# One product of weights with float32 operands, and float64 weights converted by a scale

## The chip, the cores and the metric

The kernel runs on one core of a Trainium2 chip. The metric is the device time of one execution in microseconds (us). It was executed three times for its time, and once more under the hardware profiler.

## What is computed

Causal attention with a bias from a running sum (4 batches, 8 heads, 576 positions, head dimension 64), then a gated layer, then a layer whose second half is normalised and mixed over positions:

```python
x = softmax(scale * q @ k.T + bias) @ v          # 32 heads, gathered to (4, 576, 512)
gate = sigmoid(conv over 5 positions of x)       # conv_w
x = (gate * (x @ w_val)) @ w_out                 # both 512 x 512
h = relu(x @ w_in)                               # w_in is 512 x 1024
u, v = h[..., :512], h[..., 512:]
out = (u * (w_spatial @ normalise(v) + b)) @ w_out2
```

Nothing stands between `w_out` and `w_in`, so the kernel computes the 512 x 1024 product w_out @ w_in once, on the chip, and uses it in place of the two. This product is called the fold here. The weight matrices w_val, conv_w, w_out, w_in and w_out2 arrive as float64 and are converted to float32 on the chip; q, k, v and the rest are float32.

## The kernel before, in words

**Order of the work.** The main loop (in the part of the code that is printed below only where it touches the change) goes over the 32 heads. For each head `scores` makes q.k in float32 (heads 0 to 7) or from split operands (heads 8 to 31), VectorE (DVE, L253) adds the mask and finds the row minimum, ScalarE (ACT, L258) takes the exponential, TensorE (PE) transposes the result (`transposes`), and `pv` multiplies by v for two heads at a time. Between these pieces the loop calls `more`, which takes the next steps from a queue: conversion of weights, the fold, and the two mixing layers of a batch, `mixing_a` and `mixing_b`. Within one engine instructions run in a fixed order. A scheduler that runs when the program is built sets this order; it is not written out by hand.

**Split operands.** A float32 matrix is split in a high part in a shorter format (`hi_of`, L93, mostly on ACT) and the rest (`lo_of`, L100, on DVE or POOL). A product then takes three matmuls per block of 128 rows, high by high, low by high and high by low (`three`, L440).

**Conversion of a float64 piece** (`from_f64`, L388). A piece is 128 x 512 numbers of 64 bits, 512 KB. A transfer issued on the SP queue brings it as pairs of 32-bit words. ACT (L404) takes the absolute value of the upper word, read as float32, times 65536. DVE clamps it (L405), masks the sign out of the upper word (L406), and shifts and joins (L407). GpSimd (POOL) scales the lower word (L410) and adds (L411). There are 20 such pieces, four each of w_out, of the two halves of w_in, of w_val and of w_out2, and one small one of conv_w.

**The fold.** `fold_prep` (L415) converts a piece of w_out (j is None) or of half j of w_in and splits it: `wo_h`, `wo_l`, `wih`, `wil`, one ACT instruction and one DVE instruction each. The two halves of w_in share one buffer for each part. `fold(ec, j)` (L452) makes a 128 x 512 block of the product by `three`, 12 matmuls, and splits it into `wch` and `wcl`. There are eight such blocks. Half 1 is prepared in heads 2 to 6 and multiplied in heads 7 to 9, half 0 is multiplied in heads 13 and 14.

**What sets the pace around the change.** `first_steps` (L653) puts the steps in order: conv_w, w_out, half 1 of w_in, w_val, then the four folds of half 1; `second_steps` prepares half 0 next to `mixing_b(0)`; `third_steps` prepares w_out2 and w_spatial. Loads of later heads, of weights and of weight blocks written back to memory all go through the SP queue in order.

Of the kernel before, what the change touches and what calls it, by code (L numbers as in the profile page):

```python
# [7 lines left out]
F32 = mybir.dt.float32  # L8
F32R = mybir.dt.float32r
I32 = mybir.dt.int32  # L10
U32 = mybir.dt.uint32
AF = mybir.ActivationFunctionType
ALU = mybir.AluOpType
# [3 lines left out]
NATIVE = 8  # L17


F64_LOW = 2.0 ** (896 // 8 - 127 + 16)  # L20
F64_HIGH = 2.0 ** (1150 // 8 - 127 + 16) * (1.0 + 6.0 / 8 + (1.0 - 2.0 ** -20) / 8)


@with_exitstack
def tile_stickbreak_attention_moe(
# [22 lines left out]
    NP = H // 2  # L48
# [16 lines left out]
    V, G, A, SY = nc.vector, nc.gpsimd, nc.scalar, nc.sync  # L65
# [21 lines left out]
    def f(ap):  # L87
        return ap.bitcast(F32)

    def hi_of(eng, out_, in_):  # L90

        if eng is A:
            A.activation(out_, in_, AF.Copy)  # L93
        elif eng is G:
            G.tensor_scalar(out=out_, in0=in_, scalar1=1.0, scalar2=1.0, op0=ALU.mult, op1=ALU.mult)
        else:
            V.tensor_copy(out_, in_)

    def lo_of(eng, out_, in_, hi):
        eng.tensor_tensor(out=out_, in0=in_, in1=f(hi), op=ALU.subtract)  # L100
# [21 lines left out]
    for c in (0, 128):  # L122
        n = 128 if c == 0 else 64
# [30 lines left out]
    def tmp(name, dt=F32):  # L154
        return mid.tile([128, S], dt, tag="tmp", name=name, bufs=2)
# [129 lines left out]
    def evac_split(dst_hi, dst_lo, src):  # L285
        A.activation(dst_hi, src, AF.Copy)
        lo_of(V, dst_lo, src, dst_hi)
# [45 lines left out]
    def conv(b, p):  # L333
# [5 lines left out]
        for k in range(3, -1, -1):  # L339
# [7 lines left out]
    wtmp = wtmp_cm.__enter__()  # L347
# [7 lines left out]
                         op1=ALU.max)  # L355
# [11 lines left out]
    SY.dma_start(cum_d[:, 0, :], f(ch))  # L367
    SY.dma_start(cum_d[:, 1, :], f(cl))

    wo_h = wtmp.tile([128, NP, 512], F32R, name="wo_h")  # L370
    wo_l = wtmp.tile([128, NP, 512], F32R, name="wo_l")
    wi = {}


# [10 lines left out]
                return fn(*a)  # L385
        return g

    def from_f64(src, n):  # L388

        k = count[0] % 5  # L390
        count[0] += 1
        if count[0] <= 13 and k < 3:
            if k == 0 and "g" not in W:
                W["g"] = mid.tile([128, NP * (2 * S + 64)], I32, tag="g", name="wg")
            r = W["g"][:, k * 1536:k * 1536 + 1024]
            a = f(W["g"][:, k * 1536 + 1024:k * 1536 + 1536])
        else:
            r = mid.tile([128, 1024], I32, tag="wr", name="wr", bufs=2)
            a = tmp("wa")
        W["r"] = r  # L400
        r, a = r.rearrange("p (c t) -> p c t", t=2)[:, 0:n, :], a[:, 0:n]
        SY.dma_start(r, src.rearrange("p (c t) -> p c t", t=2))
        up, low = r[:, :, 1], r[:, :, 0]
        A.activation(a, f(up), AF.Abs, scale=65536.0)  # L404
        V.tensor_scalar(out=a, in0=a, scalar1=F64_HIGH, scalar2=F64_LOW, op0=ALU.min, op1=ALU.max)  # L405
        V.tensor_scalar(out=up, in0=up, scalar1=-2 ** 31, scalar2=None, op0=ALU.bitwise_and)  # L406
        V.scalar_tensor_tensor(out=up, in0=a.bitcast(I32), scalar=3, in1=up, op0=ALU.logical_shift_left,  # L407
                               op1=ALU.bitwise_or)

        G.tensor_scalar(out=low, in0=low.bitcast(U32), scalar1=2.0 ** -29, scalar2=None, op0=ALU.mult)  # L410
        G.tensor_tensor(out=a.bitcast(I32), in0=low, in1=up, op=ALU.add)  # L411
        return a

    @paced
    def fold_prep(kc, j):  # L415

        if j is None:
            wh, wl, src = wo_h, wo_l, woT[:, kc * 1024:(kc + 1) * 1024]
        else:
            if j not in wi:  # L420
                wi[j] = [wtmp.tile([128, NP, 512], F32R, tag=f"wi{x}", name=f"wi{x}") for x in "hl"]
            wh, wl = wi[j]
            src = w_in[:, kc, j * 1024:(j + 1) * 1024]
        t = from_f64(src, 512)
        hi_of(A, wh[:, kc, :], t)
        lo_of(V, wl[:, kc, :], t, wh[:, kc, :])

    @paced
    def weight_prep(src, dst, mc):
        t = from_f64(src[mc], 512)  # L430
        w = W["r"].rearrange("p (t c) -> p t c", t=2).bitcast(F32R)
        if dst is wv_d and mc < 2:
            w = mid.tile([128, 2, 4, 128], F32R, tag="wv", name="wv", bufs=2)
            AHEAD[False, 0, mc] = w[:, 0], w[:, 1]
            w = w.rearrange("p t k m -> p t (k m)")
        hi_of(A, w[:, 0, :], t)
        lo_of(V, w[:, 1, :], t, w[:, 0, :])
        SY.dma_start(dst[mc], f(w))

    def three(pt, kcs, hl_a, hl_b):  # L440

        n = len(kcs)
        for j, kc in enumerate(kcs):
            ah, al = hl_a(kc)
            bh, bl = hl_b(kc)
            T.matmul(pt, ah, bh, start=j == 0, stop=False)
            T.matmul(pt, al, bh, start=False, stop=False)
            T.matmul(pt, ah, bl, start=False, stop=j == n - 1)

    KC = list(range(NP))  # L450

    def fold(ec, j):  # L452
        pt = ps.tile([128, 512], F32, tag="m", name="psm", bufs=2)
        es = slice(ec * 128, (ec + 1) * 128)
        cs = slice(j * 512, (j + 1) * 512)
        three(pt, KC, lambda kc: (wo_h[:, kc, es], wo_l[:, kc, es]), lambda kc: (wi[j][0][:, kc, :], wi[j][1][:, kc, :]))
        evac_split(wch[:, ec, cs], wcl[:, ec, cs], pt)


# [193 lines left out]
    def first_steps():  # L653
        nonlocal cw
        cw = early.tile([128, NP, 5], F32, name="cw")
        V.tensor_copy(cw, from_f64(conv_w, 20).rearrange("p (c k) -> p c k", k=5))
        order = [(lambda mc=mc: weight_prep(w_val, wv_d, mc)) for mc in KC]
        order += [(lambda mc=mc: fold_prep(mc, None)) for mc in KC]
        order = order[4:] + [(lambda kc=kc: fold_prep(kc, 1)) for kc in KC] + order[:4]
        for o in order:  # L660
            o()
            yield
        for ec in range(4):
            fold(ec, 1)
            yield 2.56

    def second_steps():
        for kc in KC:
            fold_prep(kc, 0)
            yield  # L670
# [11 lines left out]
    def start():  # L682

        m = mixing_a(0)
        yield from both(m, first, 2)
        m = mixing_b(0)
        yield from both((next(m) for _ in range(5)), second_steps())
        for ec in range(4):
            fold(ec, 0)
            yield 2.56  # L690
        open_late()
        yield from both((next(m) for _ in range(8)), third_steps())
        yield from m
# [117 lines left out]
```

## Time and profile before

| | before |
|---|---|
| median of three executions | 500.99 us (500.11 to 503.02) |
| profiled execution, its own time | 502.31 us |
| its span in the trace | 500.5 us |
| PE busy | 474.9 us, 95% |
| DVE busy | 320.2 us, 64% |
| ACT busy | 315.4 us, 63% |
| POOL busy | 165.8 us, 33% |
| granted TensorE clock, mean | 0.993 of full speed |

The span is the profiled execution from its first to its last instruction; the profiled execution's own time is 1.81 us more than its span, and 1.32 us more than the median. Busy time of PE includes the time that a matmul takes to run through the array, so that its 95% is not 95% of what it could do. The trace is read here in stages that are cut where the scores of a head begin on PE: head 2 at 21.38 us, head 8 at 79.59, head 15 at 167.22, head 22 at 271.76 and head 31 at 379.71 us. In these stages the engines stand against each other in different ways, which the shares over the whole span do not show. PEclk is the granted clock, where 1.00 is TensorE's higher level, 2.4 GHz, and its lower level is 1.2 GHz.

### The profile page before, as it was taken

To read this page: it belongs to the slowest core of one execution; us is meant where nothing else is said; L and a number is where in the kernel's file an instruction comes from. 1 tells how busy PE (TensorE), PEld (TensorE's weight loads), DVE (VectorE), ACT (ScalarE), POOL (GpSimd) and SP (SyncE) were. 2 spreads that over 40 slices of the span, in tenths; PEclk is the share of its full clock that TensorE was granted. 3 is DMA by queue.
4 is the path that set the end of the run, shared out by engine and by line. 5 is a ranking of instruction groups with operands and counts; after the bars stand their busy time and mean duration, and the time that the engine had idled before them with its cause. 6 is when DMAs were issued, how large, how long until landed. Compare 5 with 4: busy or idle time off the path is not lost.

```text
span 500.5 us, 9139 instructions
## 1 busy us (share of the span) xinstructions
PE 474.9 (95%) x3138; PEld 400.7 (80%) x3138; DVE 320.2 (64%) x835; ACT 315.4 (63%) x796; POOL 165.8 (33%) x183
## 2 busy tenths in 40 slices
PE   8697789979999999999999999999999999999997
PEld 5453457768777898998879999888778989988997
DVE  5599999698989885655578476555794453124120
ACT  2787968786776876675577758674876624234322
POOL 5587452045583103103243023012342022136130
PEclk9898999999999999999999999999999999999999
DMA  3876477558383644287531412784510072600002
GB/s 93 223 250 209 108 256 252 158 158 236 118 265 113 182 128 123 76 252 231 145 88 43 130 47 80 230 249 129 168 42 28 0 279 54 211 1 2 0 13 84
DMA packets 51567, 68.23 MB, mean 136 GB/s; under 512 B 23936, under 2 KB 39456, under 8 KB 51520
## 3 DMA queue, kind: packets, MB, share of 16 engines
q1 hardware_dynamic: 46592, 62.84, 42.3%
q10 hardware_dynamic: 4928, 4.80, 2.9%
q8 instruction: 25, 0.41, 0.4%
q14 instruction: 22, 0.18, 0.1%
HBM read 54.91 MB, written 9.16 MB: 128 GB/s over the span
## 4 chain that ended last, share of the span: by engine, by line
PE 63%; DVE 20%; DMA 7%; ACT 3%; issue 3%; POOL 2%; SPq 1%; DVEq 0%; ACTq 0%; POOLq 0%
PE psm L75 45%; PE pso L75 5%; PE pst L75 5%; DVE p L253 4%; DVE z L341 3%; DMA wv<-wv_d 2%; PE pss L244 2%; DMA raw<-in_qk 2%; PE pss L245 2%; DVE v L583 2%; PE psw L75 1%; DVE qk L100 1%; DVE wg L407 1%; ACT p L258 1%; PE pss L242 1%
## 5 line engine op out<-in xcount | busy, mean ns | idle before, releaser
L258 ACT ACTIVATE p<-p,nm 64x64 f32<-64x64 f32 (+4 forms) x160 | 88.5, 554 | 22.6 <-DVE nm L253 22.2
L253 DVE CUSTOM_DVE_ANT_0 p<-pss,mask 64x64 f32<-64x64 f32 (+4 forms) x160 | 62.7, 412 | 25.1 <-PE pss L245 17.7
L301 ACT ACTIVATE pt<-pst 128x512 f32<-128x512 f32 (+2 forms) x128 | 59.0, 495 | 28.3 <-PE pst L75 28.1
L341 DVE SCALAR_TENSOR_TENSOR z<-x,cw,z 128x575 f32<-128x575 f32 (+1 forms) x64 | 57.3, 896 | 7.4 <-ACT z L338 7.1
L75 PE MATMUL pst<-ident,p 128*128 128x128 f32 x416 | 60.1, 276 | 2.0 <-ACT p L258 1.8
L100 POOL TENSOR_TENSOR y<-gt,y 128x288 fp32r<-128x288 f32 x32 | 27.1, 847 | 102.8 <-ACT y L93 102.8
L100 POOL TENSOR_TENSOR g<-gt,g 128x288 fp32r<-128x288 f32 x32 | 28.8, 903 | 95.0 <-ACT g L93 94.7
L75 PEld LDWEIGHTS pst<-ident,p 128*128 128x128 f32 x416 | 48.4, 141 | 11.2 <-ACT p L258 4.3
L75 PE MATMUL psm<-g,wch 128*128 128x288 f32 x256 | 55.1, 299 | 1.2 <-DVE wcl L100 0.9
L75 PE MATMUL pso<-pt,vraw 128*64 128x512 f32 (+4 forms) x320 | 52.1, 448 | 0.0
L75 PE MATMUL psm<-wch,g 128*128 128x512 f32 x144 | 47.7, 400 | 0.0
L244 PE MATMUL pss<-qk 128*64 128x64 f32 (+1 forms) x144 | 43.6, 320 | 2.7 <-DVE nm L253 2.3
L75 PEld LDWEIGHTS psm<-g,wch 128*128 128x128 f32 x256 | 42.4, 189 | 2.0 <-DVE wcl L100 1.2
L75 PE MATMUL psm<-y,wv 128*128 128x288 f32 x288 | 42.0, 297 | 0.5 <-ACT ot L629 0.5
L75 PE MATMUL psm<-xvh,wv 128*128 128x288 f32 x192 | 40.2, 300 | 1.7 <-DMA wv<-wv_d 1.3
L245 PE MATMUL pss<-kd,cn 66*64 66x64 f32 (+1 forms) x144 | 41.1, 294 | 0.0
L242 PE MATMUL pss<-raw 128*128 128x320 f32 (+4 forms) x96 | 31.5, 432 | 9.6 <-DVE nm L253 6.0
L75 PEld LDWEIGHTS psm<-y,wv 128*128 128x128 f32 x288 | 39.6, 188 | 0.9 <-ACT ot L629 0.7
L524 DVE TENSOR_TENSOR gt<-psm,u 128x288 f32<-128x288 f32 x32 | 14.5, 456 | 39.3 <-PE psm L75 31.2
L75 PEld LDWEIGHTS pso<-pt,vraw 128*64 128x64 f32 (+1 forms) x320 | 19.3, 138 | 23.4 <-issue 16.7
L75 PE MATMUL psm<-wsh,vh 128*128 128x288 f32 x128 | 38.0, 299 | 0.0
L75 PE MATMUL psm<-g,wcl 128*128 128x288 f32 x128 | 38.0, 297 | 0.0
(142 smaller groups left out, 1118.9 us busy)
## 6 DMA issues: line engine op xcount, KB each, us to landing
raw<-in_qk SPq DMA_DIRECT2D x24, 448.0 KB
wv<-wo_d SPq DMA_DIRECT2D x12, 512.0 KB
R<-r_d SPq DMA_DIRECT2D x32, 160.0 KB
wv<-wv_d SPq DMA_DIRECT2D x10, 512.0 KB
out<-ot ACTq DMA_DIRECT2D x32, 144.0 KB
vraw<-in_vp SPq DMA_DIRECT2D x32, 128.0 KB
cn<-qk SPq DMA_DIRECT2D x24, 144.0 KB
raw<-in_qk SPq DMA_DIRECT2D x48, 64.0 KB
```

The lines of the kernel that those rows point to most:

```text
L75: m = op(*a, **k)
L100: eng.tensor_tensor(out=out_, in0=in_, in1=f(hi), op=ALU.subtract)
L242: nc.tensor.matmul(pst[0:m, o:o + b - a], r[:, 1, q0:q0 + m], r[:, 0, k0 + a:k0 + b], start=True, stop=True)
L244: nc.tensor.matmul(pst[0:m, o:o + b - a], qa[:, q0:q0 + m], kb[:, k0 + a:k0 + b], start=True, stop=False)
L245: nc.tensor.matmul(pst[0:m, o:o + b - a], qc[0:KD, q0:q0 + m], kd[0:KD, k0 + a:k0 + b], start=False, stop=True)
L253: LAST["V"] = V.tensor_tensor_reduce(out=row[:, a:b], in0=src, in1=mask[0:m, o:o + b - a], scale=-0.125, scalar=3.0e38 if a == 0 else nm[0 ...
L258: A.activation(row, row, AF.Exp, bias=nm[0:m, i:i + 1], scale=-1.0, accum_out=sm[h // 2 % 2][0:m, h % 2, i:i + 1])
L301: A.activation(PT[h][:, to:to + n], pt[:, o:o + n], AF.Copy)
L341: V.scalar_tensor_tensor(out=z[:, d:], in0=x[:, :S - d], scalar=cw[:, p, k:k + 1], in1=z[:, d:], op0=ALU.mult, op1=ALU.add)
L407: V.scalar_tensor_tensor(out=up, in0=a.bitcast(I32), scalar=3, in1=up, op0=ALU.logical_shift_left, op1=ALU.bitwise_or)
L524: V.tensor_tensor(out=t, in0=psrc, in1=other, op=ALU.mult)
L583: V.tensor_scalar(out=v[0:m], in0=v[0:m], scalar1=mv[0:m, 0:1], scalar2=rs[0:m], op0=ALU.subtract, op1=ALU.mult)
```

## The change

The fold's operands stay float32, `wo_f` and `wi[j]`, with no split: each block of the product is made by 4 float32 matmuls in place of 12 on split operands. The two halves of w_in have a buffer each. A converted piece of these matrices is built directly in its place (`home`). In `from_f64`, for all 20 pieces, ACT multiplies the upper word by 2**-112 with its sign kept, and the clamp on DVE is gone: one DVE instruction masks and shifts, a second one joins the sign. POOL's two instructions and the transfers stay as they were.

```diff
-F64_LOW = 2.0 ** (896 // 8 - 127 + 16)
-F64_HIGH = 2.0 ** (1150 // 8 - 127 + 16) * (1.0 + 6.0 / 8 + (1.0 - 2.0 ** -20) / 8)
+F64_SCALE = 2.0 ** -(896 // 8)
...
-    wo_h = wtmp.tile([128, NP, 512], F32R, name="wo_h")
-    wo_l = wtmp.tile([128, NP, 512], F32R, name="wo_l")
+    wo_f = wtmp.tile([128, NP, 512], F32, name="wo_f")
...
-    def from_f64(src, n):
+    def from_f64(src, n, home=None):
...
-            a = tmp("wa")
+            a = tmp("wa") if home is None else None
+        if home is not None:
+            a = home
...
-        A.activation(a, f(up), AF.Abs, scale=65536.0)
-        V.tensor_scalar(out=a, in0=a, scalar1=F64_HIGH, scalar2=F64_LOW, op0=ALU.min, op1=ALU.max)
-        V.tensor_scalar(out=up, in0=up, scalar1=-2 ** 31, scalar2=None, op0=ALU.bitwise_and)
-        V.scalar_tensor_tensor(out=up, in0=a.bitcast(I32), scalar=3, in1=up, op0=ALU.logical_shift_left,
-                               op1=ALU.bitwise_or)
+        A.activation(a, f(up), AF.Copy, scale=F64_SCALE)
+        ai = a.bitcast(I32)
+        V.tensor_scalar(out=up, in0=ai, scalar1=0x0FFFFFFF, scalar2=3, op0=ALU.bitwise_and, op1=ALU.logical_shift_left)
+        V.scalar_tensor_tensor(out=up, in0=ai, scalar=-2 ** 31, in1=up, op0=ALU.bitwise_and, op1=ALU.bitwise_or)
...
     def fold_prep(kc, j):
...
-            wh, wl, src = wo_h, wo_l, woT[:, kc * 1024:(kc + 1) * 1024]
+            home, src = wo_f, woT[:, kc * 1024:(kc + 1) * 1024]
...
-                wi[j] = [wtmp.tile([128, NP, 512], F32R, tag=f"wi{x}", name=f"wi{x}") for x in "hl"]
-            wh, wl = wi[j]
-            src = w_in[:, kc, j * 1024:(j + 1) * 1024]
-        t = from_f64(src, 512)
-        hi_of(A, wh[:, kc, :], t)
-        lo_of(V, wl[:, kc, :], t, wh[:, kc, :])
+                wi[j] = wtmp.tile([128, NP, 512], F32, name=f"wi{j}")
+            home, src = wi[j], w_in[:, kc, j * 1024:(j + 1) * 1024]
+        from_f64(src, 512, home[:, kc, :])
...
-        three(pt, KC, lambda kc: (wo_h[:, kc, es], wo_l[:, kc, es]), lambda kc: (wi[j][0][:, kc, :], wi[j][1][:, kc, :]))
+        for kc in KC:
+            T.matmul(pt, wo_f[:, kc, es], wi[j][:, kc, :], start=kc == 0, stop=kc == NP - 1)
```

The scheduler sets a new order on every engine. Two places matter below. The rows give line, operation, result<-operands and shape, in the order of one engine; the line of a statement is up to four lower in the changed code (L253 is L252, L438 is L434).

**DVE at the end of head 2** (`p`, `nm` and `pss` belong to the scores; `wg`, `wr` and `wa` to a piece that is being converted; `wo_` to w_out). Before:

```order
L266 TENSOR_SCALAR den<-sm_121 128x10
L253 ISA p_125,nm<-pss,mask 128x256
L253 ISA nm 128x1
L268 RECIPROCAL rin<-den 128x10
L405 TENSOR_SCALAR wa<-wa 128x512
L406 TENSOR_SCALAR wr<-wr 128x512
L100 TENSOR_TENSOR wo_l<-wg,wo_h 128x512
L253 ISA p_125,nm<-pss,mask,nm 128x320
```

The same place with the change:

```order
L265 TENSOR_SCALAR den<-sm_121 128x10
L252 ISA p_125,nm<-pss,mask 128x256
L252 ISA nm 128x1
L267 RECIPROCAL rin<-den 128x10
L406 TENSOR_SCALAR wr<-wo_f 128x512
L407 SCALAR_TENSOR_TENSOR wr<-wo_f,wr 128x512
L252 ISA p_125,nm<-pss,mask,nm 128x320
```

Ahead of the last reduction of the head the clamp (L405) and the low part (L100) are gone, and the joining instruction (L407), which came behind that reduction before, has moved up.

**The SP queue around the second load of head 11** (`raw_67`). Before:

```order
L438 DMA wv_d<-wg 128x1024
L202 DMA cn_116<-qk 64x576
L175 DMA raw_67<-in_qk 128x2x448
L177 DMA raw_67<-in_qk 128x2x64
L178 DMA raw_67<-in_qk 128x2x64
```

With the change:

```order
L434 DMA wv_d<-wg 128x1024
L201 DMA cn_116<-qk 64x576
L402 DMA wr<-in_w_in 128x1024
L174 DMA raw_67<-in_qk 128x2x448
L176 DMA raw_67<-in_qk 128x2x64
```

The fourth and last load of half 0 of w_in now stands directly ahead of the load of this head; before, it came 15 entries later.

## Rows read from the trace of the kernel before

**Rows 1.** the page's head, busy us and slices of 12.5 us in tenths
```profile
PE 474.9 (95%) x3138; PEld 400.7 (80%) x3138; DVE 320.2 (64%) x835; ACT 315.4 (63%) x796; POOL 165.8 (33%) x183
...
PE   8697789979999999999999999999999999999997
...
DVE  5599999698989885655578476555794453124120
```

**Rows 2.** windows, all engines: stretch, length, busy (instructions), then clock, DMA share, GB/s
```profile
21.38:79.59 58.21, 49.92 (x249) 29.41 (x250) 55.54 (x145) 46.59 (x122) 38.06 (x27) 0.94 0.65 202
79.59:167.22 87.63, 81.94 (x500) 65.54 (x499) 77.92 (x196) 67.66 (x168) 36.70 (x33) 1.00 0.60 182
167.22:271.76 104.54, 103.33 (x739) 91.36 (x738) 68.14 (x177) 69.80 (x178) 25.23 (x30) 1.00 0.50 145
271.76:379.71 107.95, 106.94 (x766) 94.25 (x765) 70.35 (x200) 77.11 (x205) 25.15 (x30) 1.00 0.44 129
379.71:500.50 120.79, 117.17 (x837) 109.75 (x834) 35.88 (x79) 44.48 (x101) 30.01 (x40) 1.00 0.21 68
```

**Rows 3.** waits of PE, 21.38 to 79.59: us in total, times, longest
```profile
PE pss L242 <- DVE nm L253: 5.8, 8, 1.3
PE pss L242 <- DMA raw<-in_qk: 3.4, 1, 3.4
PE psq L75 <- ACT rt L275: 1.4, 1, 1.4
PE psr L75 <- DVE rin L268: 0.7, 1, 0.7
```

**Rows 4.** chain of waits, 0 to 160 us: start, us, what
```profile
27.02 0.73 DVE wa L405
...
28.10 0.60 DVE wo_l L100
28.70 0.46 DVE p L253
```

**Rows 5.** groups of DVE instructions, 21.38 to 79.59 us
```profile
L405 DVE TENSOR_SCALAR wg<-wg 128x512 f32<-128x512 f32 x7 | 4.3, 612 | 0.0
...
L405 DVE TENSOR_SCALAR wa<-wa 128x512 f32<-128x512 f32 x5 | 3.4, 672 | 0.2 <-ACT wa L404 0.2
...
L100 DVE TENSOR_TENSOR wil<-wg,wih 128x512 fp32r<-128x512 f32 x3 | 2.0, 680 | 0.0
...
L100 DVE TENSOR_TENSOR wo_l<-wg,wo_h 128x512 fp32r<-128x512 f32 x2 | 1.7, 844 | 0.0
...
L100 DVE TENSOR_TENSOR wo_l<-wa,wo_h 128x512 fp32r<-128x512 f32 x2 | 1.4, 679 | 0.0
...
L100 DVE TENSOR_TENSOR wil<-wa,wih 128x512 fp32r<-128x512 f32 x1 | 0.7, 672 | 0.0
```

**Rows 6.** timeline of PE in head 7: start, us, line, operation, tiles, count
```profile
71.39 1.09 PE L75 MATMUL pst<-ident,p 128*128 128x128 f32 x8
72.32 0.92 PE L242 MATMUL pss<-raw 128*128 128x448 f32 x2
72.72 0.75 PE L75 MATMUL psm<-wih,wo_h 128*128 128x512 f32 x1
...
75.61 0.40 PE L75 MATMUL psm<-wil,wo_h 128*128 128x512 f32 x1
```

**Rows 7.** windows, columns as in Rows 2
```profile
40.00:50.00 10.00, 7.83 (x34) 3.45 (x32) 10.00 (x27) 7.82 (x21) 7.56 (x6) 0.83 0.64 218
```

**Rows 8.** groups of DVE instructions, 79.59 to 271.76 us
```profile
L100 DVE TENSOR_TENSOR wil<-wa,wih 128x512 fp32r<-128x512 f32 x4 | 3.0, 745 | 1.8 <-PE pst L75 1.8
...
L405 DVE TENSOR_SCALAR wa<-wa 128x512 f32<-128x512 f32 x7 | 2.9, 419 | 1.0 <-ACT wa L404 1.0
```

**Rows 9.** tile wr: minimum/median/maximum ns of each group
```profile
L406 DVE TENSOR_SCALAR wr<-wr x10: 387/427/1265, 27.7 to 137.2; 128x512 int32<-128x512 int32 x10
```

**Rows 10.** groups of ACT instructions, 21.38 to 79.59 us
```profile
L93 ACT ACTIVATE wih<-wg 128x512 fp32r<-128x512 f32 x3 | 1.9, 617 | 0.0
```

## Prediction

> **What bounds the kernel now.** I read the page's busy shares first and then its slices. PE is busy 95% of the span, so PE looks like the bound everywhere; but in the slices PE is below 9 tenths in most of the first ten, and there DVE stands at 9 [rows 1]. The next view is the table of stages, cut at the heads. From head 2 to head 8 (58.21 us) PE is busy 49.92 us and idle 8.29, while DVE is busy 55.54. From head 8 to head 15 (87.63 us) PE is idle 5.69 and DVE busy 77.92. From head 15 to head 22 PE is idle 1.21 of 104.54 us, and from there to head 31 1.01 of 107.95 [rows 2]. So there are two regimes: until head 8 DVE sets the pace, from head 15 on PE does, and between them both nearly do. The waits of PE in the first stage say the same: 5.8 us on the row minimum that DVE makes, in 8 waits, 1.4 and 0.7 us on ACT and DVE steps of the sums; the 3.4 us on a load end where the stage begins and are none of its time [rows 3]. The chain of waits runs there from one DVE instruction to the next, and among them are the ones that this change removes: a clamp (L405) and a low part (L100) right ahead of a score's reduction (L253) [rows 4]. Since PE is the bound later, a microsecond that heads 2 to 15 arrive earlier is a microsecond off the end, and so is one that PE gets in addition.
>
> **What the change removes from DVE.** In the stage from head 2 to head 8 there are 12 clamps, 4.3 + 3.4 = 7.7 us, and eight low parts, 2.0 + 1.7 + 1.4 + 0.7 = 5.8 us [rows 5]: 13.5 of 55.54 us. From head 8 on there are seven clamps, 2.9 us, and four low parts, 3.0 us [rows 8]: 5.9 of 77.92 us. (One more clamp of full size lies ahead of head 2, and that of conv_w is 20 numbers wide; both count for nothing.) The two DVE instructions that stay are of the kinds that were there. The one that now masks and shifts took between 387 and 1265 ns, with 427 in the middle, in its old form [rows 9]; the new form has two operations and other operands, and the trace does not show it. I take the same price; if each of 20 ran at the upper end, that would be 20 x 0.84 = 17 us of DVE, nearly all that was saved, and if each ran at the lower end, 1 us less. The middle is nearest, for it is the same kind of instruction, one input and no second tensor.
>
> **What it removes from ACT and POOL.** ACT loses twelve high parts of 0.617 us [rows 10], 7.4 us in all; two thirds lie in the first stage, where ACT is busy 46.59 of 58.21 us [rows 2]. It is not the longest there, so I count nothing for this by itself: the cover is DVE and PE, and if both got shorter than ACT, ACT's 42 us would still not be the longest. POOL's work is the same. Its last add now ends a piece, while before an ACT and a DVE instruction followed; no one waits for the pieces in the first stage, so this is counted at nothing too.
>
> **What it adds on PE.** Twelve split matmuls of 512 columns become four float32 ones. Of the split ones, the first ends at 72.72 + 0.75 = 73.47 us and the twelfth at 75.61 + 0.40 = 76.01; between them are 11 steps, so one is 0.231 us and a block 2.77 [rows 6]. A float32 matmul shows as two records. The one of 448 columns just ahead ends at 72.32 + 0.92 = 73.24, and the transposes before it at 71.39 + 1.09 = 72.48: 0.76 us, for 512 columns 0.87, for a block of four 3.47 [rows 6]. So a block costs 0.70 us more, eight of them 5.6. If a float32 matmul took four steps of 0.231, it would be 0.92, a block 3.70 and eight blocks 7.4 us more. A gain is excluded, as 3.47 is the lowest that the float32 rows give. I take 5.6, from the row of the same type of operand. Two blocks (1.4 us) come ahead of head 8, as before, and six (4.2 us) in the next stage. There the extra evacuation is none: ACT and DVE split a block into wch and wcl as before.
>
> **What is moved.** The last load of half 0 of w_in now stands on SP directly ahead of a load of head 11, behind which further loads queue. It waits for POOL to free a buffer. POOL was busy 36.70 of 87.63 us in that stage [rows 2] and takes that piece a head earlier than before, so I count nothing; without that cover a late load costs PE what the one of head 2 did, 3.4 us [rows 3]. The halves of w_in no longer share a buffer, so the second half's pieces need not wait for the folds of the first. That can only spread work.
>
> **The sum.** In the first stage PE can get back 8.29 us of idle time, and some time of its clock: between 40 and 50 us the granted clock is 0.83, a loss of 1.7 us [rows 7], after PE had waited again and again. That is 10.0 us. DVE's relief of 13.5 us is more than this, but PE also waits on round trips, from score to reduction and back, that a free DVE shortens and does not remove. I take 60%, 6.0 us, less 1.4 for two blocks: -4.6. In the second stage 5.69 us of idle time stand against 5.9 us of relief on DVE; I take half, 2.8, less 4.2 for six blocks: +1.4. After that PE has no idle time worth counting and the work is the same: 0. Together -3.2 us. The profiled execution took 502.31 us, 1.32 above the median, so it would take 499.1, and the median would be 500.99 - 3.2 = **497.8 us**.
>
> **A rule that speaks against it.** By the span's row PE is the busiest engine, at 95% against 64% of DVE [rows 1]. The Trainium skill, Perfetto Trace Analysis, section Identifying the Most-Contended Engine, says to improve the engine with the highest occupancy first; a change that loads that engine to relieve a lesser one goes against this. By that rule none of the idle time comes back, and the time would be 500.99 + 5.6 = 506.6 us; by the stages it is 497.8. The trace bears the rule out from head 15 on, and not before head 8. The same page's section Optimization Strategy grants that the most-contended engine can change over time.
>
> **The rivals.**
> - *PE pays and gets little back* (slower). PE's waits on the row minimum are round trips between engines and not a backlog of DVE, and the freed time goes idle on DVE. For it: DVE waited only little for anything, yet in the second stage PE is busy 81.94 of 87.63 us with 4.2 us added. Against it: DVE's 55.54 of 58.21 us [rows 2]. It decides if less than 3.1 of the 15.7 us (10.0 + 5.7) come back; with none, 506.6, with 2 us, 504.6.
> - *The gain and the price cancel* (within 0.5%). Between 3.1 and 8.1 us come back, as when loads on SP and ACT's 42 us take the place of DVE after the first few microseconds. With half of the first stage's idle time without its clock, 4.1, and a third of the second's, 1.9: 500.99 + 5.6 - 6.0 = 500.6.
> - *DVE was the whole bound* (faster). All of 10.0 us come back in the first stage and 4 in the second: 500.99 + 5.6 - 14.0 = 492.6. For it: the chain through DVE alone [rows 4].
> - That the change does not do what it says is excluded by the order of DVE: clamps and low parts are gone from it.
>
> **How the numbers follow.** 0.5%, 2.5 us, is about what a measurement of this kernel can tell from no change. The forecast, with 494 to 498.5 as its own range, gets 0.38, the whole bound 0.15, the cancelling case 0.33, the slower one 0.14. So faster by over 0.5% is 0.53, within 0.5% 0.33, slower 0.14. The range runs from 492.5, the whole bound, to 504.0, which takes in the cancelling case, the dearer blocks (1.8 us more) and half of the slower case; some 0.17 is left out.
>
> **What would show it.** Head 8 should start near 75 us and head 22 near 268.5; eight blocks should show 64 float32 records and end 3.5 us after they begin when nothing comes between. DVE's busy time should fall by some 19 us to 301, PE's rise by 5 to 6 us to 480. PE's idle time between heads 2 and 8 should be about 4 us. The prediction is wrong if head 8 starts later than 78 us (the idle time was round trips), if the new masking instruction takes over 0.8 us, or if a gain at head 8 is lost again by head 22.

## The result, and the profile after

The changed kernel takes **508.09 us** (median of 6 executions, 506.28 to 509.61), the kernel before in the same session 502.70 us (6 executions, 500.11 to 503.39). The ratio is 1.0128 with a 95% interval of 1.0098 to 1.0158: 1.3% slower, some 6.4 us, where 3.2 us less was forecast, and outside the range. (The two medians alone differ by 5.4 us, 1.1%, which lies within the interval.) Medians are over all executions; the ratios leave out the few that ran over 1.5% longer than the fastest of their kernel. The profiled execution took 509.16 us and its span is 507.4 us, 6.9 us longer than before. The mean granted clock is 0.993 in both.

The busy times on the page of the changed kernel, and its slices (12.7 us each), against [rows 1]:

```profile
PE 479.3 (94%) x3106; PEld 393.8 (78%) x3106; DVE 306.3 (60%) x802; ACT 309.2 (61%) x784; POOL 161.9 (32%) x183
...
PE   8698799799999999978999999999999999999997
```

PE does 4.4 us more, DVE 13.9 and ACT 6.2 us less. What to see lies in the slices: before, PE stands at 9 from the tenth slice on, the last one apart; now there is a dip to 7 and 8 in the eighteenth and nineteenth, at 216 to 241 us, far behind everything that the change touches.

The table of stages, cut at the starts of heads 2, 8, 15, 22 and 31 on PE, against [rows 2]; columns are stretch, length, busy time of PE, PEld, DVE, ACT and POOL, clock, DMA share, GB/s:

```profile
21.50:77.19 55.69, 50.16 (x240) 28.07 (x241) 46.63 (x127) 43.32 (x115) 35.20 (x27) 0.94 0.70 211
77.19:171.38 94.19, 89.03 (x509) 64.94 (x508) 73.94 (x187) 67.42 (x169) 35.82 (x35) 1.00 0.57 171
171.38:278.83 107.45, 101.27 (x713) 87.59 (x712) 67.70 (x174) 67.26 (x174) 25.19 (x30) 1.00 0.48 140
278.83:385.70 106.87, 106.16 (x760) 93.43 (x759) 69.50 (x198) 76.91 (x204) 25.41 (x30) 1.00 0.45 130
385.70:507.40 121.70, 117.66 (x837) 109.86 (x834) 36.81 (x79) 44.47 (x101) 29.65 (x40) 1.00 0.21 67
```

Length minus busy time of PE is its idle time. From head 2 to head 8 it is 5.53 us (before 8.29), from head 8 to 15 5.16 (5.69), **from head 15 to 22 6.18 (1.21)**, then 0.71 and 4.04 (1.01 and 3.62). Head 22 starts 7.1 us later than before (278.83 against 271.76), and from there to the end both take the same time (228.6 and 228.7 us). Up to head 22 PE has the same work in both, but for the product and six mixing matmuls (0.8 us) that now come ahead of head 22. So the 7.1 us come apart into 5.3 us more of busy time (240.46 against 235.19), 1.7 us more of idle time (16.87 against 15.19) and 0.1 ahead of head 2. The idle time of the first stage did fall by 2.8 us; the third stage gave 5.0 us back. (The lengths of the second and third stage alone can't be set against those before, because 4.7 us of mixing matmuls stand ahead of head 15 now that stood behind it.)

The waits of PE from 171 to 279 us in the changed kernel; columns are the wait, us in total, times, longest:

```profile
PE psm L74 <- DMA wv<-wv_d: 2.5, 2, 2.3
PE psm L74 <- DMA wv<-wo_d: 2.0, 1, 2.0
PE pss L243 <- DVE nm L252: 0.6, 2, 0.4
PE psm L74 <- ACT ot L626: 0.6, 1, 0.6
```

The same view of the kernel before, 167 to 272 us:

```profile
PE psm L75 <- DMA wv<-wv_d: 1.0, 1, 1.0
PE psm L75 <- ACT u L602: 0.3, 1, 0.3
```

The new idle time is waiting for weight blocks of the mixing layers, `wv`, 512 KB each, that come back from memory through the SP queue into two buffers. Where it stands, the timeline of PE tells, and under it that of SP's issues (start, length, line, what, and in brackets the idle time before and what ended it):

```profile
218.51 0.20 PE L243 MATMUL pss<-qk 128*64 128x64 f32 x1
...
221.86 5.00 PE L74 MATMUL psm<-y,wv 128*128 128x288 f32 x36 [1.99 <-DMA wv<-wo_d]
...
235.90 0.50 PE L74 MATMUL psm<-xvh,wv 128*128 128x288 f32 x2 [2.33 <-DMA wv<-wv_d]
```

```profile
216.12 2.63 SPq L503 DMA_DIRECT2D wv<-wo_d  x2
...
225.31 4.17 SPq L503 DMA_DIRECT2D wv<-wv_d  x2
...
233.60 6.72 SPq L503 DMA_DIRECT2D wv<-wv_d  x2
```

Head 19 starts at 218.51 us, head 20 at 249.64, 31.1 us later; before, the two starts are 10.05 us apart (223.15 and 233.20). Between them the scheduler has now put 17.4 us of mixing matmuls (counted along PE's order, at the trace's durations); before, no head has more than 12. I call this heap of mixing work **the bunch**. A weight block is used up in about 3.2 us there, and the next can be issued only when one of two buffers is free; spread over the heads the loads are hidden, in a bunch they are not. The windows of this head (all engines, then the matmuls into `psm` alone) show it:

```profile
218.51:249.64 31.13, 26.38 (x197) 23.43 (x195) 10.36 (x30) 13.09 (x35) 5.42 (x6) 1.00 0.68 205
```

```profile
218.51:249.64 31.13, 19.26 (x132) 17.82 (x132) 3.17 (x7) 1.97 (x5) 1.00 0.68 205
```

There is a second new wait, in the stage from head 8 to head 15. The longest wait of PE there, and what DVE and SP did at that time:

```profile
98.80 0.54 PE L74 MATMUL psm<-xvh,wv 128*128 128x288 f32 x2 [2.76 <-DVE wcl L99]
```

```profile
97.26 0.56 DVE L325 TENSOR_TENSOR x<-pso,R 128x384 f32<-128x384 f32 x1 [4.45 <-DMA R<-r_d]
...
98.06 0.68 DVE L99 TENSOR_TENSOR wcl<-psm,wch 128x512 fp32r<-128x512 f32 x1
```

```profile
91.90 0.47 SPq L281 DMA_DIRECT2D R<-r_d  x1
92.46 0.54 SPq L182 DMA_DIRECT2D vraw<-in_vp  x1
93.05 0.64 SPq L183 DMA_DIRECT2D vraw<-in_vp  x1
93.75 0.59 SPq L281 DMA_DIRECT2D R<-r_d  x1
```

`wcl` empties the `psm` buffer of the last block of half 1, and the mixing matmul needs that buffer. In DVE's order a step on the attention output (`x`, L325) stands ahead of `wcl`, and it waits 4.45 us for the row sums `R`, which make a round trip through memory. Their second half is issued 1.85 us after the first, with two loads of `vraw` between; before, the two stand back to back there (95.53 us, x2) and the same step waits 0.81 us. The order of DVE has turned round as well: before, the `wcl` of the same block stood ahead of that step, so that a late load of `R` could not hold the buffer.

```profile
97.11 0.69 DVE L100 TENSOR_TENSOR wcl<-psm,wch 128x512 fp32r<-128x512 f32 x1
...
99.48 0.56 DVE L326 TENSOR_TENSOR x<-pso,R 128x384 f32<-128x384 f32 x1 [0.81 <-DMA R<-r_d]
```

What the change itself costs is as summed. A row of the chain of waits, a block of the product with nothing between:

```profile
142.79 3.44 PE psm L74 x8
```

### The profile page after: what moved, and what is told of

Same layout as the page of the kernel before. It is cut to its first block, busy times and chain, and to the rows that moved or that the text cites. A ratio compares the mean times of both kernels' runs of the same rounds, so it can differ in the third digit from the quotient of the medians.

```text
span 507.4 us, 9047 instructions
## 1 busy us (share of the span) xinstructions
PE 479.3 (94%) x3106; PEld 393.8 (78%) x3106; DVE 306.3 (60%) x802; ACT 309.2 (61%) x784; POOL 161.9 (32%) x183
## 4 chain that ended last, share of the span: by engine, by line
PE 73%; DMA 10%; DVE 8%; ACT 3%; issue 2%; POOL 2%; SPq 1%; DVEq 0%; POOLq 0%; ACTq 0%
PE psm L74 49%; PE pso L74 8%; PE pst L74 7%; PE pss L241 3%; PE pss L243 3%; DMA raw<-in_qk 3%; PE pss L244 3%; DVE p L252 2%; DMA out<-ot 2%; DVE z L340 1%; DMA wv<-wv_d 1%; DMA wv<-wo_d 1%; DMA wsr<-in_wsT 1%; DVE qk L99 1%; ACT pt L300 1%
## 5 line engine op out<-in xcount | busy, mean ns | idle before, releaser
L252 DVE CUSTOM_DVE_ANT_0 p<-pss,mask 64x64 f32<-64x64 f32 (+4 forms) x160 | 62.4, 412 | 22.8 <-PE pss L244 14.2
L340 DVE SCALAR_TENSOR_TENSOR z<-x,cw,z 128x575 f32<-128x575 f32 (+1 forms) x64 | 56.1, 876 | 7.4 <-ACT z L337 7.0
L74 PE MATMUL pso<-pt,vraw 128*64 128x512 f32 (+4 forms) x320 | 50.4, 437 | 0.2
L243 PE MATMUL pss<-qk 128*64 128x64 f32 (+1 forms) x144 | 45.0, 333 | 3.0 <-DVE nm L252 3.0
L519 DVE SCALAR_TENSOR_TENSOR gt<-z,psm 128x288 f32<-128x288 f32 x32 | 14.4, 449 | 44.8 <-PE psm L74 43.6
L74 PE MATMUL psm<-wsl,vh 128*128 128x288 f32 x128 | 37.7, 296 | 0.0
```

The source lines that it names most:

```text
L74: m = op(*a, **k)
L243: nc.tensor.matmul(pst[0:m, o:o + b - a], qa[:, q0:q0 + m], kb[:, k0 + a:k0 + b], start=True, stop=False)
L252: LAST["V"] = V.tensor_tensor_reduce(out=row[:, a:b], in0=src, in1=mask[0:m, o:o + b - a], scale=-0.125, scalar=3.0e38 if a == 0 else nm[0 ...
L340: V.scalar_tensor_tensor(out=z[:, d:], in0=x[:, :S - d], scalar=cw[:, p, k:k + 1], in1=z[:, d:], op0=ALU.mult, op1=ALU.add)
L519: V.scalar_tensor_tensor(out=t, in0=other, scalar=more, in1=psrc, op0=ALU.add, op1=ALU.mult)
```

## The experiments

Two theories went into the runs. **A**: the price of the float32 blocks is paid whole, and the relief of DVE brings next to nothing. **B**: the relief is worth several microseconds at the front, and they are lost again between heads 15 and 22, where the new order bunches mixing work that waits for its weights. All runs were timed in five rounds against the kernel before on the same chip; ratios are to it. The groups of runs stood on different chips, so that runs of different groups are compared by their ratios. In the diffs "before" and "after" are the two kernels of this document.

### One part alone: the conversion

Before, with the `from_f64` part of the change only (scale on ACT, mask and shift on DVE, no clamp); product and split stay.

```diff
-        A.activation(a, f(up), AF.Abs, scale=65536.0)
-        V.tensor_scalar(out=a, in0=a, scalar1=F64_HIGH, scalar2=F64_LOW, op0=ALU.min, op1=ALU.max)
...
+        A.activation(a, f(up), AF.Copy, scale=F64_SCALE)
```

> The kernel before with the new conversion alone (scale by 2**-112, no clamp); the product of w_out and w_in stays split, so PE's work is the old one. Theory A (the price of the float32 blocks on PE is all paid and DVE's relief brings next to nothing back): 501 to 503.5 us, as before at 502.7. Theory B (the relief is worth several us, and the changed kernel lost them again between heads 15 and 22, where its order puts mixing work in a bunch that waits for weight loads): 497 to 499.5 us, PE idle time from head 2 to head 8 down by 3 us or more.

Measured: 502.61 us, 1.0015 [0.9989, 1.0041]: no difference, as A said; B missed. Part of the reason is again the order: the scheduler moved the blocks of half 1 behind head 8, so head 8 starts at 74.07 us with 5.4 us less of PE's work ahead of it, and head 22 at 272.07, as before. From head 2 (20.18 us) to head 8 PE is still idle 10.1 us, 8.1 of them in five waits on the row minimum, the longest 3.2 us. Taking work off DVE did not by itself shorten PE's waits for DVE here.

### The other part alone: the product

After, with the old conversion.

```diff
-        A.activation(a, f(up), AF.Copy, scale=F64_SCALE)
...
+        A.activation(a, f(up), AF.Abs, scale=65536.0)
+        V.tensor_scalar(out=a, in0=a, scalar1=F64_HIGH, scalar2=F64_LOW, op0=ALU.min, op1=ALU.max)
```

> The changed kernel with the old conversion (absolute value and clamp): only the float32 product. Its order has no bunch of mixing work in head 19. Theory A: eight blocks of 0.7 us more, 506 to 509 us. Theory B: without the bunch the changed kernel's 5 us of idle time between heads 15 and 22 are not there, and the low parts are gone from DVE: 503 to 505.5 us. Both: a block of eight float32 records takes 3.4 to 3.5 us.

Measured: 513.32 us, 1.0220 [1.0184, 1.0255], more than either theory allowed. No line of its trace is read here, and the cause of its 11 us stays open.

### Holding the order of PE

The loop has a switch that makes PE follow the order of the program instead of the scheduler's; it is on from head 18 to head 31. Moving its start moves what the scheduler may bunch. First, from head 9 on, in both kernels:

```diff
-        chain[0] = 18 <= w < 32
+        chain[0] = 9 <= w < 32
```

> The kernel before with the matmuls of mixing, fold, transposes and p.v held in the order of the program from head 9 on (the flag that does this from head 18 on is set earlier). It is the partner of the next run, whose order on PE is then the same from head 15 on. The time itself is not forecast better than 498 to 510 us.

> The changed kernel with the same flag from head 9 on, to be compared with the run before it. Theory A (price of the blocks): 5 to 6.5 us slower than that run. Theory B (the loss lies in the order that the scheduler chose): 0 to 3 us slower, and no idle time of several us of PE on weight loads between heads 15 and 22.

Measured: before 514.15 us, 1.0267 [1.0228, 1.0305], above the 498 to 510 expected; after 511.79 us, 1.0191 [1.0157, 1.0224]. In this order, which from head 9 on is the program's in both kernels, the change is 2.4 us *faster* by the medians and 3.8 by the ratios. A had it 5 to 6.5 us slower and falls in its strict form; B (0 to 3 slower) is nearer and misses too. The order itself costs the kernel before some 13 us and the changed one some 3 (1.0191 less 1.0128): from 70 to 180 us PE is busy 99.6 and 101.5 of 110 us, at a clock of 0.94.

Then later starts, to take the bunch away without touching the front (the order of PE is the same as in after up to head 15):

```diff
-        chain[0] = 18 <= w < 32
+        chain[0] = 16 <= w < 32
```

(and 17 or 19 in place of 16).

> The kernel before with the matmuls of mixing, transposes and p.v held in the program's order from head 16 on, not 18. From head 18 on its order on PE is word for word that of the next run. Theory B (a bunch of mixing work in one head costs PE waits on weight loads) and theory A (the price of the blocks alone): both 500 to 505 us, since it has no bunch of more than 14 us in a head and no change of the product.

> The changed kernel with the order held from head 16 on. Up to head 15 it is the changed kernel as it was; the bunch of 17 us of mixing work between heads 19 and 20 is gone. Theory A: 507 to 510 us, 5 to 6 us above the run before it. Theory B: 502 to 505 us, PE idle time from head 15 to head 22 down from 6.2 us to 3 or less.

> The same with the order held from head 17 on, another order without the bunch (10, 10 and 11 us of mixing work ahead of heads 18, 19 and 20). Theory A: 507 to 510 us. Theory B: 502 to 505 us.

> The same with the order held from head 19 on: the bunch is there, 16.5 us in one head, one head later than in the changed kernel. Theory A: 507 to 510 us. Theory B: as the changed kernel, 506.5 to 510 us, with several us of waits of PE on weight loads around that head.

| | time, us | ratio | bunch, us of mixing in one head | waits on wv, us |
|---|---|---|---|---|
| before, from 16 | 502.11 | 1.0006 [0.9982, 1.0029] | none | none |
| after, from 16 | 509.39 | 1.0155 [1.0120, 1.0191] | none | 1.3 |
| after, from 17 | 503.82 | 1.0031 [1.0008, 1.0055] | none | 1.3 |
| after (18) | 508.09 | 1.0128 [1.0098, 1.0158] | 17.4 | 4.5 |
| after, from 19 | 508.14 | 1.0115 [1.0075, 1.0154] | 16.5 | 5.2 |

The waits are from 160 us to the start of head 22 or a little behind it; the kernel before, in its own order, has 1.0. The waits of PE of the last one, 190 to 290 us:

```profile
PE psm L74 <- DMA wv<-wv_d: 3.2, 2, 1.7
PE psm L74 <- DMA wv<-wo_d: 2.0, 1, 2.0
```

and of the order from 17, 169 to 290 us:

```profile
PE psm L74 <- DMA wv<-wv_d: 1.3, 1, 1.3
PE pss L243 <- DVE nm L252: 0.9, 1, 0.9
```

From 17 to 19 nothing but the order differs; the bunch comes back, the waits on `wv` grow by 3.9 us, and the time by 0.84%, 4.2 us. (The two ratios are known to 0.24% and 0.4%.) The order from 17 is B's case, that from 19 fits both. The order from 16 is B's miss: no bunch, 1.3 us of waits on `wv`, and still the slowest of the four, in the range that A gave. In its trace, just after head 16 (windows of 3 us, the clock is the number ahead of the last two):

```profile
186.00:189.00 3.00, 1.34 (x5) 0.91 (x5) 2.94 (x11) 1.38 (x7) 0.00 (x0) 0.86 0.48 138
189.00:192.00 3.00, 2.96 (x12) 2.58 (x12) 2.35 (x8) 2.68 (x9) 1.14 (x2) 0.50 0.24 59
192.00:195.00 3.00, 3.00 (x14) 3.00 (x14) 0.46 (x1) 0.44 (x1) 0.55 (x2) 0.50 0.00 0
195.00:198.00 3.00, 3.00 (x26) 2.97 (x25) 1.01 (x3) 1.49 (x5) 1.37 (x2) 1.00 0.02 5
```

PE waits 1.66 us at once for DVE there, and for almost 7 us after it the granted clock is 0.50 (1.2 GHz), in which mixing matmuls start 0.24 us apart that start 0.13 apart at 2.4 GHz: some 3 us lost. The order from 17 has a drop at the same place, but a shorter one:

```profile
187.00:190.00 3.00, 3.00 (x16) 2.75 (x16) 2.94 (x12) 2.32 (x8) 0.00 (x0) 0.53 0.74 193
```

That one is back at 1.00 after 3.4 us and loses 1.7 us, so that this place makes up less than 2 of the 5.6 us between the two runs. By the mean clock of all their executions, 0.986 against 0.991, the clock makes up about half of them, as an estimate. The rest stays open.

### Taking the bunch's wait away

After, with every second late weight block loaded into the two `wr` buffers, which stand empty once the weights are converted: four buffers in place of two. The order on PE is the same up to head 15. Behind it the scheduler has set another one: head 19 has 94 mixing matmuls, some 13 us, where the changed kernel has 132, 17.4 us.

```diff
+        if home == "wr":
+            w = mid.tile([128, 1024], F32R, tag="wr", name="wwr", bufs=2)
...
-        return AHEAD.pop(key) if key in AHEAD else load_chunk(src, mc)
+        late = mc % 2 == 1 and (b > 0 or src is wo_d)
+        return AHEAD.pop(key) if key in AHEAD else load_chunk(src, mc, "wr" if late else "wv")
```

The second run gives the same buffers to the kernel before, as a control.

> The changed kernel with two more buffers for blocks of weights that are loaded back (the two that conversion has left free), used for every second block from the second mixing layer of batch 0 on. Theory B (the loss after head 15 is waits of PE on weight loads): 502.5 to 505.5 us, the waits on wv loads between heads 15 and 22 (4.5 us in the changed kernel) under 1 us. Theory A (price of the blocks alone): 507 to 510 us.

> The same two buffers in the kernel before, as the control. It has 1.3 us of such waits. Both theories: 500 to 502.5 us, 0 to 1.5 us faster than before. If it gains as much as the changed kernel does with them, the buffers say nothing on the change.

Measured: after with them 503.47 us, 1.0031 [1.0003, 1.0059]; before with them 502.90 us, 1.0034 [1.0010, 1.0058], if anything slower, where both theories had 500 to 502.5. So the buffers, with the order that comes with them, are worth nothing in the kernel before, and 0.97% (1.0128 less 1.0031, known to about 0.4%), 4.9 us, in the changed one. All waits of PE from 168 to 274 us in the changed kernel with them:

```profile
PE pss L243 <- DVE nm L252: 1.4, 1, 1.4
PE pst L74 <- ACT p L257: 0.3, 1, 0.3
```

and the window of most of its mixing work, columns as in the stages:

```profile
213.00:248.00 35.00, 35.00 (x262) 32.38 (x261) 18.34 (x56) 22.47 (x58) 5.65 (x7) 1.00 0.69 204
```

No wait on `wv` is left, and PE is busy in all of the 35 us. From head 15 to head 22 PE is idle 1.76 us, 4.4 less than in the changed kernel (6.18). Because the order changed along with the buffers, the run takes the waits and part of the bunch away together and does not tell them apart. But an order alone brings the same back: from 17 to 19 it was 4.2 us. So B's main claim is shown in this form: **4 to 5 of the some 6 us go with the bunch and its waits for weight loads**, each of the two differences being known to about 2 us. With the buffers the two kernels are equal (503.47 and 502.90).

### What the product's matmuls are worth

After, with the product's sum cut short: two matmuls per block in place of four.

```diff
-        for kc in KC:
-            T.matmul(pt, wo_f[:, kc, es], wi[j][:, kc, :], start=kc == 0, stop=kc == NP - 1)
+        for kc in KC[:2]:
+            T.matmul(pt, wo_f[:, kc, es], wi[j][:, kc, :], start=kc == 0, stop=kc == 1)
```

> The changed kernel with the product made from the first 256 of the 512 rows alone (two of four float32 matmuls in a block): PE has 16 x 0.87 = 13.9 us less to do, and the bunch of mixing work between heads 19 and 20 is the same. Theory A: PE's time goes to the end one for one, 493 to 496 us. Theory B as well, if PE is the bound in heads 8 to 15; if other engines were the bound there, less than half of it shows, 501 us or more.

Measured: 502.67 us, 1.0018 [0.9982, 1.0054]. A said 493 to 496 and missed. Of B's two cases the second, in which PE is not the bound in heads 8 to 15, holds in its numbers: PE had 13.9 us less to do, and the time fell by 5.5 by the ratios, some four tenths. The mean clock of its executions was 0.982 against 0.990 of the changed kernel, and from head 8 to head 15 PE is idle 9.90 us, where the changed kernel has 5.16. More than half of that is one wait, of PE on an exponential of ACT; and ACT had a piece of w_in ahead of it, whose transfer it waited for:

```profile
99.71 1.33 PE L74 MATMUL pst<-ident,p 128*128 128x128 f32 x5 [5.44 <-ACT p L257]
```

```profile
98.24 0.65 ACT L404 ACTIVATE wi<-wr 128x512 f32<-128x512 f32 x1 [5.10 <-DMA wr<-in_w_in]
```

Work that leaves PE at the front comes back in part as idle time and as a lower clock.

### The price of the product in one order

Conversion alone with the buffers; then that with the order from 17; then the whole change with buffers and the order from 17. The last two have the same order on PE from head 19 on and no bunch. Ahead of head 17 their orders differ: with the split product the blocks of half 1 come behind head 8, as in the conversion alone.

```diff
-        chain[0] = 18 <= w < 32
+        chain[0] = 17 <= w < 32
```

> The new conversion with the old split product, and the two buffers. Theory A: 501 to 503 us, as the conversion alone. Theory B: 1 us below that at most, since the conversion alone shows only 0.5 us of waits on these loads: 500 to 502.5 us.

> New conversion, split product, the two more buffers, order held from head 17 on. From head 19 on its order on PE is that of the next run. 498 to 502 us, near the run without the held order (499.8), if the order from head 17 on costs nothing where no weight load is waited for.

> The changed kernel with the two more buffers and the order held from head 17 on; against the run before it only the product differs. If the blocks' price of 5.6 us is partly paid back by the relief of DVE and ACT from low and high parts: 1.5 to 4.5 us above that run. If it is paid in full: 5 to 6.5 us above. If it is paid back in full: within 1 us.

Measured: conversion with buffers 499.80 us, 0.9986 [0.9959, 1.0012], just below what either theory had; in the order from 17 500.78 us, 0.9987 [0.9962, 1.0012]; the whole change 504.22 us, 1.0058 [1.0035, 1.0081]. So the conversion is worth nothing that can be measured, by itself or with buffers, and the product with float32 operands costs 3.4 us net (3.6 by the ratios), each of the two times being known to about 1.2 us. That is less than its price of 5.6, and it takes in what the different order of the front does. What that net cost consists of, the waits suggest. The two longest waits of PE from 80 us on, first of the whole change, then of the conversion, both in the order from 17:

```profile
PE psm L74 <- DVE wcl L99: 3.4, 1, 3.4
PE pss L243 <- DVE nm L252: 2.9, 4, 1.4
```

```profile
PE pss L243 <- DVE nm L252: 1.8, 3, 1.5
PE psm L74 <- ACT u L606: 1.2, 2, 0.7
```

The wait on `wcl` behind the row sums is there, 3.4 us just ahead of head 10, in the kernel with the float32 product and not in the other. So have the traces of all six kernels of the whole change whose loop keeps the scheduler's order up to head 15 (2.6 to 3.4 us); those with the split product have no wait on `wcl` between 76 and 150 us of over 0.9 us. That this wait makes up the net cost is a reading of traces: a run that lets the row sums come earlier was not made.

No version beats both kernels: the conversion with more buffers has the lowest median, 499.80 us, but its interval includes 1.

## Why the prediction was wrong

**Right: the price.** A block was to take 3.47 us and takes 3.44, so eight cost about the 5.6 us of the sum; PE's busy time was to be 480 us and is 479.3, and up to head 22 it has 5.3 us more. DVE was to fall to 301 and fell to 306.3. The new mask and shift is not to blame: L406 takes 10.9 us in all, against 12.7 before. But DVE's splitting step `kd`, which the change does not touch, takes 21.2 us in its 24 instructions where it took 17.8 (885 ns each against 743); why, was not tried.

**Right in size, though not in this trace, and with other parts: the first stage.** Head 8 was to start near 75 us. In the profiled execution it starts at 77.19; the six kernels that share this order of PE up to head 15 start it at 77.19, 75.77, 75.43, 74.83, 74.21 and 73.38 (median 75.1), and three of the old front at 79.87, 79.59 and 78.0. So about 4.5 us are gained there, with two dearer blocks paid, where 4.6 were forecast. The mechanism of the sum is seen in the waits of PE from head 2 to head 8 in the changed kernel: those on the row minimum went from 5.8 us [rows 3] to 2.8.

```profile
PE pss L241 <- DVE nm L252: 2.8, 5, 1.0
```

But PE's idle time there was to be about 4 us and is 5.53, and 5.0 to 6.5 in the six; the rest of the gain came from the clock. The three traces of the old front have two drops of the clock (to 0.50 for 3.4 us) each in this stage; of the six new ones those that start head 8 at 77.19 and 75.77 have two, those at 75.43 and 74.21 one, those at 74.83 and 73.38 none. Each trace is one execution, so part of the match with 75 is luck. With the conversion alone the waits on the row minimum did not fall, though two blocks had moved out of that stage as well.

**Wrong: "In the second stage ... I take half, 2.8".** PE's idle time fell from 5.69 to 5.16 us (4.9 to 5.6 in the six traces of the new front, 4.2 to 6.1 in the three of the old). PE stood ready for the first mixing matmul of `xvh` at 96.0 us, which ran at 98.3 before, and there the next thing was late: the row sums, whose round trip the change does not shorten, whose second load the new order put behind two others, and behind which it put `wcl` on DVE. A wait of 2.76 us, where none before was over 1.2, took the place of those that went. The sum looked for what is late next at the load of head 11 and at the pieces of weights, where no wait of PE came, and not here. (One of the seven clamps that it counts in this stage, 0.4 us, lies behind head 15.)

**Wrong, and the main step: "After that PE has no idle time worth counting and the work is the same: 0".** The work is the same and its order is not. With the front shorter on DVE and the fold longer on PE, the scheduler placed the mixing steps of heads 15 to 22 anew, heaped 17.4 us of them into head 19, and PE waited for their weights: 5.0 us more idle time in that stage. The prediction looked at the new order around heads 2 and 11 only, and took the regime "PE is the bound" from [rows 2] as a property of the stage, where it was one of the order in that stage. The buffers and the order that came with them take the wait away and give 4.9 us back, about half of the 9.6 us by which the sum was off. Of the three signs of being wrong that the prediction named, this is the last: the gain at head 8 was lost again by head 22, which starts at 278.83 us and was to start near 268.5.

**The rivals.** "PE pays and gets little back" gave 506.6 us, and the rule of the Trainium skill (Perfetto Trace Analysis, section Identifying the Most-Contended Engine) gave the same; the measured time is 1.5 us above. In number they were nearest. As a mechanism they did not hold in the first stage: the relief did reach head 8, and what ate it was a wait for transfers and one for a round trip, which neither names. Without the bunch's wait, and the order from 16 apart, the whole change stands at 1.003 to 1.006 of before, nearest to the rival in which gain and price cancel.

**How the difference between forecast (-3.2) and result (+6.4) comes apart**, by the profiled executions, whose spans differ by 6.9 us, so that 10.1 are to be told: 5.0 us of idle time behind head 15, 2.3 us in the second stage that were not recovered, 2.2 us at head 8, which was 77.19 in this execution in place of 75, and 0.6 in smaller pieces.

## What to carry to other kernels

Where a scheduler sets the order, an edit can move the order of stages that it does not touch: count, per stage and along the bound engine's order, how much work of each kind stands between two marks, and compare both kernels there before writing a 0. That PE hardly waited behind head 15 belonged to one order of its work and loads; ask what a heap of that work would wait for. To price an edit apart from the order that comes with it, hold the order in both kernels, or take away the wait that the new order brought and give the old kernel the same as a control. Then compare the orders of these runs too: here the added buffers changed the order again.

## What the runs showed of the hardware that was not expected

Each of the two profiled executions has two drops to 0.50 for about 3.4 us, a loss of 1.7 us each, after PE had waited repeatedly; they lie near 22 and 46 us before and near 24 and 58 us after, so in these two the change moved one and removed none, and the 1.7 us of clock that the first stage was to give back [rows 7] did not come. In four of the other five traces of the new front it did, with one drop there or none. The windows of after that hold them (columns as in the stages):

```profile
20.00:30.00 10.00, 8.50 (x35) 5.34 (x35) 6.40 (x25) 8.21 (x21) 7.08 (x6) 0.83 0.75 243
...
50.00:60.00 10.00, 7.58 (x29) 4.40 (x28) 9.51 (x27) 6.61 (x19) 3.52 (x3) 0.84 0.53 152
```

In the order from 16 a single wait of 1.66 us stood ahead of almost 7 us at the lower level; at the same place the order from 17 and the kernel with more buffers have 3.4 us of it, and the changed kernel none. The mean clock over all executions of a kernel differs too: 0.991 for before, 0.986 for the order from 16, 0.982 with half the product and 0.979 for before in the order from 9. The changed kernel has 0.990, so that the clock accounts for little of its loss. What decides whether a wait is followed by a drop, these runs do not show.
